# Attention scores with a stationary operand of 128 columns, and products of ones on TensorE until batch 0 is through

## The chip, the cores and the metric

The kernel runs on one core of a Trainium2 chip. The metric is the device time of one execution in microseconds (us). TensorE (PE in the profile) multiplies matrices: it loads a stationary operand (a row of its own, PEld) and streams a moving operand past it, into PSUM. VectorE (DVE), ScalarE (ACT) and GpSimd (POOL) do the rest, and DMA queues move data.

## The reference

For 8 batches, 12 heads, 448 positions and 64 elements per head: cosine attention, then a mixing block on the 448 x 768 result of each batch.

```python
q_n = q / (norm(q) + 1e-6);  k_n = k / (norm(k) + 1e-6)
attn = softmax(q_n @ k_n.T / tau)           # per batch and head
x = (attn @ v), heads side by side           # 448 x 768
u = x + ((x.T @ U) @ V).T                    # rank 32, over positions
out = u + relu(u @ w_ch1) @ w_ch2            # 768 -> 3072 -> 768
```

## The kernel before

All operands of products are bf16, sums are f32 in PSUM. PSUM is one tile `bank` of eight banks of 512 f32 columns. Positions are cut into four chunks of 112 (`SC`, `SCH`).

**Attention**, per batch and pair of heads (six pairs): q and k are loaded (L463), squared (L492 on ACT or L494 on DVE), summed (L498), turned into 1/norm (L511 to L519) and scaled into `xn` (L553). Batches 0 and 1 transpose `xn` on PE in groups of four chunks (`flip`, L443), with a copy of each group to `qkT` by ACT (L839) or DVE (L841); later batches use a DMA transpose. `qkT` holds 64 rows of one head and 64 of the other, eight chunks of 112 columns: four of q or k for the one side, four for the other. The scores (L587) take one chunk as the stationary operand (64 rows by 112 columns) against 448 columns of the other side, for both heads, so that a chunk is a pair of products on the two halves of the rows. Batch 0 plans them chunk by chunk, later batches in bursts of two chunks (`BURST`). ACT takes the exponential (L593) of both heads of a chunk into `attn`. The products with v (L607), 16 a head, have `attn` as the stationary operand and 65 columns of v, with a column of ones that gives the softmax's sum; DVE divides (L614, L616) into `X_sb`.

**Mixing**: X with U (L664, a stationary operand of 128 rows by 32 columns), with V (L643, L699, L745), a copy of X through PE in batch 0 (L638), then the products with the first weight matrix (L775, `w1_sb`), ReLU (L798, L800), those with the second (L809, `w2_sb`), the sum (L818) and the store (L832).

**Order.** Nothing is looped in order of batches. Every operation is an `Op` with a planned duration, dependencies and slots of rings that it takes and frees. `Plan.run` simulates the engines at build time. PE and POOL have ordered streams (for PE the streams `pe_tp`, `pe_first`, `pe_av`, `pe_a`, `pe_sc`, `pe_mlp`, in this order of preference), and whichever head is ready first in the plan is issued next; DVE, ACT and SP take by priority; copies and squares marked "ACT/DVE" go to the engine that the plan has free. So a planned duration that changes moves other work. The planned order is then the order in each engine's queue; semaphores do the waiting. PSUM banks 0 to 3 are two slots of scores (`r_sc`), banks 4 to 7 are shared by the rings `r_mm` (transposes and all mixing products, three at a time) and `r_av` (the products with v, two at a time). The first squares belong to heads 0 and 1 (on ACT), then 2 and 3, 4 to 7, 8 to 11.

Of the kernel before, what the change touches and what calls it, by code (L numbers as in the profile page):

```python
# [12 lines left out]
BF = mybir.dt.bfloat16  # L13
# [243 lines left out]
def kernel(  # L257
# [12 lines left out]
    nc = tc.nc  # L270

    B, H, S, D = q.shape
# [8 lines left out]
    SCH = S // SC  # L281
# [3 lines left out]
    PE_BATCHES = 2  # L285
    LATE, VLATE = 8.0, 3.2
    BURST = 2

    const = ctx.enter_context(tc.tile_pool(name="const", bufs=1))
    pool = ctx.enter_context(tc.tile_pool(name="pool", bufs=1))  # L290
# [58 lines left out]
    def bank_ring(groups, cap, shape=None):  # L349
        def make(g):  # L350
            if len(g) > 1:
                return bank_t[:, g[0]:g[-1] + 1, :]
            t_ = bank_t[:, g[0], :]
            if shape is not None:
                t_ = t_[:, 0:shape[0] * shape[1]].rearrange("p (a b) -> p a b", a=shape[0])
            return t_
        return BankRing(banks, groups, cap, make)

    r_mm = bank_ring([(7,), (6,), (5,), (4,)], 3)
    r_av = bank_ring([(4,), (5,), (6,), (7,)], 2, (4, D + 8))  # L360
    r_sc = bank_ring([(0, 1), (2, 3)], 2)
    r_sc1 = bank_ring([(0,), (2,), (1,), (3,)], 4)


# [17 lines left out]
        return ap.rearrange("(s c) d -> c s d", c=SC)[c, s0:s1]  # L382

    plan = Plan()
    pe_tp = plan.stream("PE")
    pe_first = plan.stream("PE")
    pe_av = plan.stream("PE")
# [5 lines left out]
    def pe_t(n):  # L393
        return n / 2400.0 + 0.0025
# [14 lines left out]
    def fill(fn, n=256, prio=8, acq=(), deps=()):  # L409
        return plan.add(Op("DVE", 0.05 + n * 0.0005, fn, deps=deps, acq=acq, prio=prio))  # L410
# [121 lines left out]
    def stats_first(ld, ops):  # L532
# [5 lines left out]
            ups.append(up)  # L538
        return ups + norm(0, 0, ld, 0, inv, 0, done, -1)

    def norm(b, p, ld, la, inv, a, deps, pr):


        by_pe = b < PE_BATCHES
        first = b == 0 and p == 0
        xn, qkT = Slot(r_xn, 2 if by_pe else 1), Slot(r_qkT, SC // (1 if b == 0 else BURST))

        def part(i):
            def fn():
                src = ld.tile[:, i, la:la + 2, :].rearrange("p h (c d) -> p h c d", d=D)  # L550
                sc = inv.tile[:, i, a:a + 2, :].unsqueeze(3).to_broadcast([SCH, 2, SC, D])
                dst = xn.tile[:, SC * (1 - i):SC * (2 - i), :].rearrange("p c (h d) -> p h c d", h=2)
                nc.vector.tensor_mul(dst, src, sc)  # L553
            return plan.add(Op("DVE", dve_t(512), fn, deps=[deps[i]], acq=[xn],
                               rel=[getattr(ld, "slot", ld), inv], prio=pr))

        ops = {i: part(i) for i in ((0, 1) if first else (1, 0))}
        if not by_pe:
            done = [plan.add(Op("SP", 0.1, lambda: nc.sync.dma_start_transpose(
                out=qkT.tile, in_=xn.tile.rearrange("p b e -> p (b e)")), deps=list(ops.values()), acq=[qkT],  # L560
                rel=[xn], prio=0, lat=("x", 0.05 * 56, LATE)))]
        else:
            done = []
            for i, o in ops.items():
                b0, b1 = SC * (1 - i), SC * (2 - i)
                done.append(flip(
                    pe_tp, [(lambda z=z: xn.tile[:, z, :]) for z in range(b0, b1)], SCH,
                    lambda: qkT.tile, (lambda t_, x, b0=b0, b1=b1: [(t_[:, b0:b1, :], x)]),
                    [o], [qkT], [xn], 1, "ACT/DVE", 0.09 if first else 0.05))
        got[b, p, "qkT"] = (qkT, done)  # L570
        return list(ops.values())


    def attention(b, p, X):
        off = PAD * (b % 2)
        qkT, qdeps = got.pop((b, p, "qkT"))
        attn = Slot(r_attn, 2)
        exps = []
        g = 1 if b == 0 else BURST
        for c0 in range(0, SC, g):  # L580
            scs = [Slot(r_sc, 1) for _ in range(g)]

            def score(scs=scs, c0=c0):
                for n, sc in enumerate(scs):
                    for hh in range(2):
                        r = slice(D * hh, D * hh + D)
                        nc.tensor.matmul(out=sc.tile[0:SCH, hh, 0:S], lhsT=qkT.tile[r, c0 + n, :],  # L587
                                         rhs=qkT.tile[r, SC:2 * SC, :].rearrange("p c s -> p (c s)"),
                                         start=True, stop=True)
            o = plan.add(Op("PE", (0.2 + pe_t(S) * g) * (1.8 if b == 0 and p < 2 else 1), score,  # L590
                            deps=qdeps, acq=scs, rel=[qkT]), pe_first if b == 0 else pe_sc)
            for n, sc in enumerate(scs):
                exps.append(plan.add(Op("ACT", act_t(2 * S, 0.08), lambda sc=sc, c=c0 + n: nc.scalar.activation(  # L593
                    out=attn.tile[:, c, :, off:off + S], in_=sc.tile[0:SCH, :, 0:S], func=AF.Exp,
                    scale=inv_tau), deps=[o], acq=[attn], rel=[sc], prio=0.1 if b == 0 else 1)))
        last_exp[b] = exps[-1]
        if b == 0 and p == 0:
            last_exp["first"] = [exps[0]]
        muls = []
        for hh in range(2):  # L600
            h = 2 * p + hh
            av, rd = Slot(r_av, 1), Slot(r_rd, 1)
            for t in range(4):
                for j in range(SC):
                    first, last = t == 0 and j == 0, t == 3 and j == SC - 1
                    def fn(t=t, j=j, h=h, hh=hh, av=av):
                        nc.tensor.matmul(  # L607
                            out=av.tile[:, t, 0:D + 1],
                            lhsT=attn.tile[:, j, hh, 128 * t:128 * (t + 1)],
                            rhs=v_t[b % 2][:, h, j, 0:D + 1], start=(j == 0), stop=(j == SC - 1))  # L610
                    o = plan.add(Op("PE", 0.09 if b == 0 and p == 0 else 0.033, fn,
                        deps=exps + got[b, h, "v"] + attn_set + [v_set[b % 2]] if first else (), acq=[av] if first else [],
                        rel=[attn] if last else []), pe_av)
            r = plan.add(Op("DVE", 0.20, lambda av=av, rd=rd: nc.vector.reciprocal(  # L614
                out=rd.tile, in_=av.tile[:, :, D:D + 1]), deps=[o], acq=[rd], prio=1))
            muls.append(plan.add(Op("DVE", dve_t(256), lambda av=av, rd=rd, h=h: nc.vector.tensor_mul(  # L616
                X.tile[:, :, h * D:(h + 1) * D], av.tile[:, :, 0:D],
                rd.tile.to_broadcast([128, 4, D])), deps=[r],
                acq=[X], rel=[av, rd], prio=1)))
        last_av[b, p] = o  # L620
        return muls
# [28 lines left out]
    def stage0(b, X, muls):  # L650
        par = b % 2
# [3 lines left out]
        A = Slot(r_A, 0)  # L655
# [3 lines left out]
        for c0, c1 in cols:  # L659
            mm = Slot(bank, 1)  # L660
            need = [m for i, m in enumerate(muls) if i * D < c1]
            for t in range(4):
                o = plan.add(Op("PE", pe_t(c1 - c0) + 0.2 if t == 0 else 0.01,
                                lambda t=t, c0=c0, c1=c1, mm=mm: nc.tensor.matmul(  # L664
                    out=mm.tile[R * t:R * (t + 1), 0:c1 - c0], lhsT=U_sb[:, par, t, :],
                    rhs=X.tile[:, t, c0:c1], start=True, stop=True),
                    deps=need + consts[:2 + par] if t == 0 else (), acq=[mm, A] if t == 0 else []),
                    pe_a if c1 < C else pe_av)
            a = Op("ACT/DVE", any_t(c1 - c0), None, deps=[o], rel=[mm], prio=0)
            a.fn = lambda a=a, c0=c0, c1=c1, mm=mm: copy_op(  # L670
                a, A.tile[:, c0:c1], mm.tile[:, 0:c1 - c0])
            a_done.append(plan.add(a))
            if b == 0:
                ut += [columns(X, A, uT, muls, cc, a) for cc in range(c0 // 128, c1 // 128)]
        tiles = range(3) if par == 0 else range(3, 7)
        n = 128 * len(tiles)
# [8 lines left out]
        for z, (c0, c1) in enumerate(cols):  # L685
            for i, t in enumerate(tiles):
# [7 lines left out]
                mm = Slot(bank, 1)  # L694
                for y, (AA, col) in enumerate(parts):
# [4 lines left out]
                        out=mm.tile[:, 0:c1 - c0], lhsT=V_sb[:, col:col + 128],  # L700
# [148 lines left out]
    def set_attn(t_):  # L849
        nc.vector.memset(t_[:, :, :, S:512].bitcast(mybir.dt.uint32), ones)  # L850

    attn_set = [fill(lambda t_=t_: set_attn(t_), 1000, prio=i - 2.5) for i, t_ in enumerate(attn_t)]

    def load_u(par):
# [89 lines left out]
        mlp(b, *state[b])  # L944

    order = plan.run()
    for o in order:
        for s in o.acq:
            if s.tile is None and not getattr(s, "own", False):
                s.tile = s.ring.make(s.group if isinstance(s.ring, BankRing) else s.i)  # L950
        o.fn()
# [33 lines left out]
```

## Time and profile before

| what | value |
|---|---|
| median of 13 runs | 602.39 us (600.6 to 603.99) |
| profiled execution | 601.95 us |
| its span in the trace | 600.1 us |
| PE busy | 581.3 us, 97% |
| DVE / ACT / POOL busy | 311.2 / 270.2 / 75.6 us |
| scores L587 | 384 products, 60.9 us busy |
| products with v, L607 | 1536 products, 60.5 us busy |
| L775 and L809 | 1152 and 1368 products, 233.4 and 231.2 us busy |

The span begins with the first instruction of any engine. A group's row in the profile names line, engine, operation, output<-inputs and shapes, then the count, busy time and mean duration of one; behind the second bar stands the idle time of the engine just ahead of the group, with what ended it. The duration of a product includes its way through the array, so products that follow one another closely overlap, and what a product costs PE is read from the distance between starts. In a timeline a row is a run of alike instructions: start, duration of the run, and how many.

### The profile page before, as it was taken

The page shows a single profiled execution, that of the slowest core. Times are in us where ns is not written, and L with a number is a line of the kernel's source. Part 1 is how long each engine was busy: PE and PEld are TensorE (multiplying, and loading weights), DVE is VectorE, ACT ScalarE, POOL GpSimd, SP SyncE. Part 2 cuts the span into 40 slices and gives each one's busy share as a digit, 9 for nine tenths or more (in the row PEclk, how much of TensorE's full clock was granted, in tenths as well). Part 3 has the DMA queues.
Part 4 walks back from the last instruction along what each step waited for, and adds up shares of the span by engine and source line. Part 5 has one row for each costly group of instructions (what it writes and reads, how often), then busy time and mean ns, then how long its engine had stood idle before and what let it go on. Part 6 is the DMA issues. An engine that isn't in the chain of part 4 may idle for free.

```text
span 600.1 us, 11347 instructions
## 1 busy us (share of the span) xinstructions
PE 581.3 (97%) x4725; PEld 328.7 (55%) x4725; DVE 311.2 (52%) x728; ACT 270.2 (45%) x425; POOL 75.6 (13%) x101
## 2 busy tenths in 40 slices
PE   3899999999999999999999999999999999999997
PEld 1555655544565555555445665555445666654565
DVE  7868949989988768767773243324320210110011
ACT  7777644566545556456661056604541024014300
POOL 6434220140310020030020000000000000000000
PEclk9999999999999999999999999999999999999999
DMA  9999993898795594895494121121002110310021
GB/s 144 212 201 193 209 130 69 134 112 121 83 172 97 88 108 63 141 127 82 61 78 82 54 58 29 26 71 40 2 1 55 51 40 1 90 43 1 0 54 54
DMA packets 132851, 50.66 MB, mean 84 GB/s; under 512 B 97728, under 2 KB 132800, under 8 KB 132800
## 3 DMA queue, kind: packets, MB, share of 16 engines
q0 software_dynamic: 71680, 25.73, 38.2%
q1 hardware_dynamic: 61056, 24.19, 20.5%
q8 instruction: 37, 0.61, 0.4%
q14 instruction: 14, 0.11, 0.1%
q10 hardware_dynamic: 64, 0.02, 0.0%
HBM read 52.25 MB, written 11.01 MB: 105 GB/s over the span
## 4 chain that ended last, share of the span: by engine, by line
PE 91%; DVE 4%; ACT 1%; DMA 1%; POOL 1%; issue 1%; DVEq 0%; POOLq 0%
PE bank L775 37%; PE bank L809 36%; PE bank L607 8%; PE bank L587 8%; PE bank L699 1%; DMA qk_nat<-in_q_dram 1%; ACT attn L593 1%; DVE xn L553 1%; PE bank L664 1%; PE bank L443 1%; POOL v_nat L472 1%; DVE u_nat L713 1%; POOL qk_nat L463 0%; DVE u_nat L710 0%; DVE relu L800 0%
## 5 line engine op out<-in xcount | busy, mean ns | idle before, releaser
L775 PE MATMUL bank<-uT,w_sb 128*128 128x512 bf16 (+1 forms) x1152 | 233.4, 353 | 1.3 <-DVE u_nat L710 0.7
L809 PE MATMUL bank<-w_sb,relu 128*128 128x384 bf16 (+1 forms) x1368 | 231.2, 323 | 0.6 <-DVE O_sb L818 0.3
L593 ACT ACTIVATE attn<-bank 112x896 bf16<-112x896 f32 x192 | 166.5, 916 | 131.7 <-PE bank L587 86.9
L809 PEld LDWEIGHTS <-relu 128*128 128x128 bf16 x1368 | 129.3, 98 | 91.5 <-issue 12.3
L775 PEld LDWEIGHTS <-w_sb 128*128 128x128 bf16 x1152 | 108.1, 98 | 111.0 <-issue 18.5
L798 ACT ACTIVATE relu<-bank 128x384 bf16<-128x384 f32 (+1 forms) x136 | 74.3, 547 | 131.8 <-PE bank L775 131.6
L818 DVE TENSOR_TENSOR O_sb<-bank,u_nat 128x384 f32<-128x384 f32 (+1 forms) x57 | 31.1, 549 | 173.2 <-PE bank L809 155.5
L498 DVE TENSOR_REDUCE ss<-sq 112x8 f32<-112x512 bf16 x96 | 63.2, 674 | 3.0 <-ACT sq L492 2.6
L587 PE MATMUL bank<-qkT 64*112 64x448 bf16 x384 | 60.9, 386 | 3.4 <-ACT attn L593 2.5
L607 PEld LDWEIGHTS <-attn 112*128 112x128 bf16 x1536 | 57.3, 99 | 11.3 <-issue 4.3
L553 DVE TENSOR_TENSOR xn<-qk_nat,inv 112x512 bf16<-112x512 bf16 x94 | 61.6, 687 | 0.2
L607 PE MATMUL bank<-v_nat,attn 112*128 112x65 bf16 x1536 | 60.5, 195 | 0.2 <-DVE uT L841 0.2
L800 DVE TENSOR_SCALAR relu<-bank 128x384 bf16<-128x384 f32 (+1 forms) x56 | 34.3, 612 | 32.1 <-PE bank L775 30.1
L616 DVE TENSOR_TENSOR X_sb<-bank,rd 128x256 bf16<-128x256 f32 x96 | 39.1, 417 | 1.5
L614 DVE RECIPROCAL rd<-bank 128x4 f32<-128x4 f32 x96 | 16.5, 176 | 42.6 <-PE bank L607 42.1
L463 POOL DMA_DIRECT2D qk_nat<-in_q_dram x24 | 17.1, 713 | 155.8 <-DVE xn L553 118.2
L472 POOL DMA_DIRECT2D v_nat<-in_v_dram x32 | 29.8, 942 | 53.0 <-PE bank L607 52.2
L494 DVE TENSOR_TENSOR sq<-qk_nat 112x512 bf16<-112x512 bf16 x88 | 34.2, 413 | 0.9 <-DMA qk_nat<-in_q_dram 0.8
L587 PEld LDWEIGHTS <-qkT 64*112 64x112 bf16 x384 | 18.7, 127 | 26.5 <-issue 22.6
L713 DVE TENSOR_TENSOR u_nat<-bank,X_sb 128x384 bf16<-128x384 f32 (+2 forms) x45 | 22.5, 526 | 17.9 <-PE bank L699 17.4
L443 PE MATMUL bank<-ident,xn 112*128 112x112 bf16 x96 | 10.3, 246 | 9.5 <-DVE xn L553 9.4
L463 POOL DMA_DIRECT2D qk_nat<-in_k_dram x24 | 16.8, 701 | 4.7 <-DMA w_sb<-in_moe_w_ch_dram 3.6
(46 smaller groups left out, 132.9 us busy)
## 6 DMA issues: line engine op xcount, KB each, us to landing
v_nat<-in_v_dram POOLq DMA_DIRECT2D x32, 168.0 KB, 6.6
qk_nat<-in_q_dram POOLq DMA_DIRECT2D x23, 224.0 KB, 6.0
qk_nat<-in_k_dram POOLq DMA_DIRECT2D x23, 224.0 KB, 6.6
w_sb<-in_moe_w_ch_dram POOLq DMA_DIRECT2D x4, 1152.0 KB, 15.4
w_sb<-in_moe_w_ch_dram POOLq DMA_DIRECT2D x8, 576.0 KB, 16.0
out_dram<-O_sb SPq DMA_DIRECT2D x15, 168.0 KB, 2.2
out_dram<-O_sb SPq DMA_DIRECT2D x16, 144.0 KB, 2.1
out_dram<-O_sb SPq DMA_DIRECT2D x16, 120.0 KB, 2.0
```

Source lines behind the costliest of these rows:

```text
L472: ops = [load(lambda c=c: nc.gpsimd.dma_start(out=v_t[b % 2][:, :, c, 0:D], in_=v[b].rearrange("h (s c) d -> c s h d", c=SC)[c]), SCH * H ...
L494: nc.vector.tensor_mul(y, x, x)
L498: lambda i=i, a0=a0, a1=a1, sq=sq: nc.vector.reduce_sum(ss.tile[:, i, a0:a1, :].rearrange("p h c -> p (h c)"), sq.tile[:, 0:a1 - a0, :].re ...
L553: nc.vector.tensor_mul(dst, src, sc)
L587: nc.tensor.matmul(out=sc.tile[0:SCH, hh, 0:S], lhsT=qkT.tile[r, c0 + n, :], rhs=qkT.tile[r, SC:2 * SC, :].rearrange("p c s -> p (c s)"), ...
L593: exps.append(plan.add(Op("ACT", act_t(2 * S, 0.08), lambda sc=sc, c=c0 + n: nc.scalar.activation(out=attn.tile[:, c, :, off:off + S], in_ ...
L607: nc.tensor.matmul(out=av.tile[:, t, 0:D + 1], lhsT=attn.tile[:, j, hh, 128 * t:128 * (t + 1)], rhs=v_t[b % 2][:, h, j, 0:D + 1], start=(j ...
L616: muls.append(plan.add(Op("DVE", dve_t(256), lambda av=av, rd=rd, h=h: nc.vector.tensor_mul(X.tile[:, :, h * D:(h + 1) * D], av.tile[:, :, ...
L775: o = plan.add(Op("PE", pe_t(n), lambda cc=cc: nc.tensor.matmul(out=mm.tile[:, 0:n], lhsT=w1_sb[:, cc, f * 128:(f + 1) * 128], rhs=uT.tile ...
L798: nc.scalar.activation(out=relu.tile[:, f, 0:n], in_=mm.tile[:, 0:n], func=AF.Relu)
L800: nc.vector.tensor_relu(out=relu.tile[:, f, 0:n], in_=mm.tile[:, 0:n])
L809: nc.tensor.matmul(out=mm.tile[:, 0:c1 - c0], lhsT=relu.tile[:, f, i * 128:(i + 1) * 128], rhs=w2_t[:, f, c0:c1], start=(f == 0), stop=(f ...
```

## The change

Three things change; everything else in the order follows from the planner.

- A score's stationary operand is 128 columns of the flat `qkT` from the chunk's first column on: 112 of the chunk, and 16 of the next one. The product writes 128 rows of PSUM instead of 112; the exponential still reads 112.
- `warm`, a 128 x 128 tile of ones set by DVE, is multiplied by itself into bank 4: 52 times as the first operation of PE's first stream (planned at 5.4 us), and, until the first product with U of batch 0, in every gap of PE's plan over 0.25 us, 70% of it at 0.056 us a product. In the built program there are 195 such products: 62 ahead of the first transpose, then groups of 7, 12, 12, 12, 5, 41, 12, 12, 4, 3, 3, 3 and 7. Bank 4 is kept by them until that product with U, and the products with v prefer banks 5 to 7.
- Planned durations lose what was added for the first pairs: transposes 0.05 us for 0.09, scores without the factor 1.8, products with v 0.033 for 0.09.

In the queues of the changed program, between the ninth and the 24th exponential of batch 0 ACT has no other work (before: three copies). Up to the end of batch 0's attention DVE has one square and three copies of `qkT` more, ACT as many less. Of the products of batch 0 with v, 30 stand in one run between the tenth and the eleventh score of the batch (before: 32), and later runs between scores have 10 to 22 (before: 14 to 18). Batches 1 to 7 have 84 bursts of four scores in both. POOL's queue is the same; in SP's some transposes change places.

```diff
+    FILL = 0.7
...
-    r_av = bank_ring([(4,), (5,), (6,), (7,)], 2, (4, D + 8))
+    r_av = bank_ring([(5,), (6,), (7,), (4,)], 2, (4, D + 8))
     r_sc = bank_ring([(0, 1), (2, 3)], 2)
+    r_warm = bank_ring([(4,)], 1)
...
+    pe_warm = plan.stream("PE")
     pe_tp = plan.stream("PE")
...
+    warm_t = const.tile([128, 128], BF, name="warm")
+    warm = Slot(r_warm, 1)
+
+    def warm_up(n):
+        for _ in range(n):
+            nc.tensor.matmul(out=warm.tile[:, 0:128], lhsT=warm_t, rhs=warm_t, start=True, stop=True)
...
-                    [o], [qkT], [xn], 1, "ACT/DVE", 0.09 if first else 0.05))
+                    [o], [qkT], [xn], 1, "ACT/DVE", 0.05))
...
+                flat = qkT.tile.rearrange("p b s -> p (b s)")
                 for n, sc in enumerate(scs):
                     for hh in range(2):
                         r = slice(D * hh, D * hh + D)
-                        nc.tensor.matmul(out=sc.tile[0:SCH, hh, 0:S], lhsT=qkT.tile[r, c0 + n, :],
+                        nc.tensor.matmul(out=sc.tile[:, hh, 0:S], lhsT=flat[r, SCH * (c0 + n):SCH * (c0 + n) + 128],
                                          rhs=qkT.tile[r, SC:2 * SC, :].rearrange("p c s -> p (c s)"),
                                          start=True, stop=True)
-            o = plan.add(Op("PE", (0.2 + pe_t(S) * g) * (1.8 if b == 0 and p < 2 else 1), score,
+            o = plan.add(Op("PE", (0.2 + pe_t(S) * g), score,
...
-                    o = plan.add(Op("PE", 0.09 if b == 0 and p == 0 else 0.033, fn,
+                    o = plan.add(Op("PE", 0.033, fn,
...
+                    rel=[warm] if b == 0 and c0 == 0 and t == 3 else []),
                     pe_a if c1 < C else pe_av)
...
+    warm_set = fill(lambda: nc.vector.memset(warm_t, 1.0), 128, prio=-20)
+    plan.add(Op("PE", 5.4, lambda: warm_up(52), deps=[warm_set], acq=[warm]), pe_warm)
...
     order = plan.run()
+    free, cool = None, False
     for o in order:
+        if o.by == "PE" and not cool:
+            if free is not None and o.start - free > 0.25:
+                warm_up(int((o.start - free - 0.12) * FILL / 0.056))
+            free, cool = o.start + o.dur, warm in o.rel
```

More of the change, by code (lines that the diff above doesn't have):

```diff
@@ L666, in stage0 @@
                     rhs=X.tile[:, t, c0:c1], start=True, stop=True),
-                    deps=need + consts[:2 + par] if t == 0 else (), acq=[mm, A] if t == 0 else []),
+                    deps=need + consts[:2 + par] if t == 0 else (), acq=[mm, A] if t == 0 else [],
+                    rel=[warm] if b == 0 and c0 == 0 and t == 3 else []),
                     pe_a if c1 < C else pe_av)
```

## The prediction

> **What bounds the kernel now.** I read the page's busy shares first, then its 40 slices, then the chain that ended last.
>
> ```profile
> PE 581.3 (97%) x4725; PEld 328.7 (55%) x4725; DVE 311.2 (52%) x728; ACT 270.2 (45%) x425; POOL 75.6 (13%) x101
> ...
> PE   3899999999999999999999999999999999999997
> ...
> PE bank L775 37%; PE bank L809 36%; PE bank L607 8%; PE bank L587 8%; PE bank L699 1%; DMA qk_nat<-in_q_dram 1%; ACT attn L593 1%; DVE xn L553 1%; PE bank L664 1%; PE bank L443 1%; POOL v_nat L472 1%; DVE u_nat L713 1%; POOL qk_nat L463 0%; DVE u_nat L710 0%; DVE relu L800 0%
> ```
>
> TensorE (PE) is busy in every slice but the first two, and the chain's large shares are its products. So from about 43 us (the first long run of L775 products) to the end, the time is the sum of what PE takes per product, and a saving there counts in full. By the list of waits for PE from 40 us on, PE waits only 0.7 + 0.3 + 0.3 + 0.2 + 0.2 + 0.2 = 1.9 us. Before 43 us another sum applies: batch 0's attention must be done before there is other work for PE.
>
> The page's clock row shows 9 from the first slice, but the groups of PE instructions, asked for 22 to 27.4 us and then for 27.4 to 30 us, show something else:
>
> ```profile
> L587 PE MATMUL bank<-qkT 64*112 64x448 bf16 x8 | 2.2, 607 | 0.0
> L607 PE MATMUL bank<-v_nat,attn 112*128 112x65 bf16 x32 | 1.9, 244 | 0.0
> ```
>
> ```profile
> L587 PE MATMUL bank<-qkT 64*112 64x448 bf16 x6 | 1.2, 393 | 0.0
> L607 PE MATMUL bank<-v_nat,attn 112*128 112x65 bf16 x26 | 1.2, 194 | 0.0
> ```
>
> The same products take 607 ns, then 393 ns. PE is slow until about 27.5 us and fast afterwards. The change's dense products end that stretch early.
>
> **Scores in the steady part.** PE's timeline around 300 us and around 136 us (start, duration, count):
>
> ```profile
> 299.72 0.38 PE L775 MATMUL bank<-uT,w_sb 128*128 128x512 bf16 x1
> 300.03 0.59 PE L587 MATMUL bank<-qkT 64*112 64x448 bf16 x4
> 300.55 3.19 PE L775 MATMUL bank<-uT,w_sb 128*128 128x512 bf16 x14
> ```
>
> ```profile
> 135.88 1.90 PE L775 MATMUL bank<-uT,w_sb 128*128 128x512 bf16 x8
> 137.71 0.35 PE L664 MATMUL bank<-X_sb,U_sb 128*32 128x384 bf16 x4
> 137.99 1.04 PE L775 MATMUL bank<-uT,w_sb 128*128 128x512 bf16 x4
> ```
>
> Fourteen L775 products of 512 columns take 3.19 us, one alone 0.38; so they start (3.19 - 0.38)/13 = 0.216 us apart. A score burst is two pairs of products of 448 columns, and the two of a pair run side by side (64 rows each). At that rate two pairs should take 2 x 0.216 x 448/512 = 0.378 us; from 300.03 to the next product they take 0.52, that is 0.142 more. And the product ahead of them holds PE for 0.31 instead of 0.216, 0.094 more. The excess of a burst is 0.236 us. Batches 1 to 7 have 7 x 6 x 2 = 84 bursts, so **19.8 us** lie in this excess. How much of it is the weight load?
>
> ```profile
> L607 PEld LDWEIGHTS <-attn 112*128 112x128 bf16 x1536 | 57.3, 99 | 11.3 <-issue 4.3
> L587 PEld LDWEIGHTS <-qkT 64*112 64x112 bf16 x384 | 18.7, 127 | 26.5 <-issue 22.6 <-ACT qkT L839 0.9 <-DVE qkT L841 0.4
> ...
> L664 PEld LDWEIGHTS <-U_sb 128*32 128x32 bf16 x72 | 1.9, 92 | 6.0 <-issue 6.0
> ```
>
> Columns: busy us, mean ns of one. A load of 128 columns (of 112 rows here) takes 99 ns, one of 112 columns 127, one of 32 columns 92. The full width is loaded in a shorter form, and the change gives the scores that width (their rows stay 64). What the long load costs is seen in L587's own durations, shortest 347 and median 393: the first pair of a burst waits for its load inside its duration, the second pair's load is hidden, 393 - 347 = 46 ns. The other 0.19 us stand ahead of the first product and behind the last. Do these go too? The L664 products say no: 8 x 0.216 = 1.73 us after 135.88 would be 137.61, and they start at 137.71, 0.10 late; 0.28 to the next product, where 384 columns need 0.162, is 0.12 of excess. Their load (92 ns) is shorter than the full one and they lose as much on both sides. What L664 and L587 share is a tile that is not the whole array (32 columns, 64 rows), and the changed scores still have 64 rows.
>
> The value I take: the full-width load leaves some 10 ns unhidden (46 less the 28 ns between the two load rows is 18; between 0 and 18), so **-35 ns a burst, 84 x 0.035 = -2.9 us**. The ends: the whole excess goes, -19.8 us; or the short form needs 128 rows as well, and 16 more columns cost (127 - 92)/80 x 16 = 7 ns, 84 x 0.007 = +0.6 us.
>
> The Trainium skill speaks on both sides, and nothing else here rests on it. "TensorE: Matmul & The Clock Gate", section "Weight-path perf modes", says that fast weight load is on when the number of weights is 128 and the type isn't FP32; the rows of 99 and 127 ns agree. "TensorEngine Tiling (Array Packing)", section "Key Properties", speaks against a large gain: "Changing tiling mode (not just tile) drains the TensorE". The 0.1 us on both sides of L664 and L587 fit a drain, and no run here separates them yet. By the second rule the sum is the one I take; if the loads alone made the excess, it would be -19.8.
>
> **The start.** What sets 43 us is ScalarE's (ACT) exponentials of batch 0, 24 in a row:
>
> ```profile
> 23.46 1.71 ACT L593 ACTIVATE attn<-bank 112x896 bf16<-112x896 f32 x2
> 26.16 0.92 ACT L593 ACTIVATE attn<-bank 112x896 bf16<-112x896 f32 x1 [0.98 <-PE bank L587]
> 26.97 0.53 ACT L839 COPY qkT<-bank 128x448 bf16<-128x448 bf16 x1
> 27.38 1.74 ACT L593 ACTIVATE attn<-bank 112x896 bf16<-112x896 f32 x2
> 28.99 0.56 ACT L839 COPY qkT<-bank 128x448 bf16<-128x448 bf16 x1
> 29.40 8.34 ACT L593 ACTIVATE attn<-bank 112x896 bf16<-112x896 f32 x10
> ```
>
> Ten take (8.34 - 0.96)/9 = 0.82 us from start to start. The ninth starts at 23.46, the 24th at 37.96: 14.5 us, where 15 x 0.82 = 12.3 would do. The 2.2 us between are a wait of 0.98 for a score that stood behind 32 slow L607 products, and copies (0.53, 0.56 and 0.50 at 37.60). In the changed order ACT has no copy between the ninth and the 24th: three qkT copies and one square have moved to VectorE (DVE), and PE is fast. Against it: the square that comes to DVE (about 0.4 us, row L494, 413 ns) stands ahead of the normalisation of heads 4 to 7, and DVE was busy 15.48 of 16.50 us from 6.9 to 23.4 us (the windows), so the ninth exponential comes some 0.4 later. And scores still stand behind L607 products in pieces of 30 and twice 22 (before: 32, then 14 to 18), 0.03 us each even when fast: some 0.5 us for these. 2.2 - 0.4 - 0.5 = **-1.3 us**. Ends: -2.2, and +0.5 if nothing comes back and DVE's extra work (three copies of 0.38 and the square, 1.55 us) finds no more cover than DVE's idle 16.50 - 15.48 = 1.02.
>
> The dense products themselves: 52 and 10 run before the first transpose, which waits for DVE until 6.90. Transposes of 112 columns are 0.093 us apart in the slow stretch, so 128 columns take 0.107; 62 x 0.107 = 6.6 us from about 1.1 us end at 7.7 if PE stays slow throughout, and before 6.9 if it turns fast halfway. At worst 0.8 us late, at nothing: the first eight exponentials have slack, since the ninth hangs on the load of heads 8 to 11, whose first square waits for its DMA until 16.01, and on DVE behind it. The 133 later products stand in gaps of PE's plan and fill 70% of each. A gap that isn't there costs up to 0.056 x 41 = 2.3 us in the longest, but it lies where PE waited for DVE (idle before L443, 9.4 us in all). All end before the first long L775 run. The memset of the ones (nearest row 98 ns, L847) lies in DVE's idle 2.64 us before 4.14; without that cover, 0.1. Bank 4 is kept from the other rings until the first U products; the three left were enough in the plan, and one wait for a bank would be 0.4 (39.37 was one of 0.25). From 43 us on the order of the work is also shuffled by the planner; the 1.9 us of waits can go or double: 0, between -1.9 and +1.9.
>
> **Sum.** The profiled execution took 601.95 us (span 600.1 and 1.85 around it), 0.44 under the median of 602.39. 601.95 - 2.9 - 1.3 = **597.8 us**. With the ends of the start and of the waits it goes from 601.95 - 2.9 - 2.2 - 1.9 = 594.9 to 601.95 - 2.9 + 0.5 + 1.9 = 601.5.
>
> **Rivals.**
> - *Width brings no short load with 64 rows.* For it: no row shows 64 rows with 128 columns. Against it: L607 with 112 rows has 99 ns, so full rows aren't needed. 601.95 - 1.3 + 0.6 = 601.3.
> - *One of the two 0.1 us sides goes too*, if it belongs to the long load: 84 x 0.096 = 8.1 more, 589.7. *Both go*: 601.95 - 19.8 - 1.3 = 580.9. L664 speaks against both.
> - *Slower: the pairs no longer run side by side.* Today the timeline shows four products in 0.52 us. If the short form keeps the second half's load from lying beside the first half's product, a pair takes another 0.187 us: 168 x 0.187 = 31.4, less 1.3 and 2.9, 629 us. It decides once (4.2 + 1.2)/0.187, about 29 of 168 pairs, run one after the other. Against it: in full tiles the short load already lies beside products (L775 at 0.216 a product).
>
> **How the numbers follow.** Forecast 0.62, no short load 0.14, one side 0.08, both sides 0.08, pairs apart 0.08. The range 589 to 602.3 holds the forecast, the one-sided case and most of the first rival, 0.81; the likeliest case's own range is 594.9 to 601.5. A measurement of this kernel can tell about 0.2% (1.2 us) from no change. Faster: 0.62 + 0.08 + 0.08 and 0.02 of the first rival, 0.80; within: 0.10 of it; slower: 0.08 + 0.02 = 0.10.
>
> **What would show it.** Score load row at about 98 ns with 128 columns; L587's successor with first pairs near 357 ns and pairs still together; excess of 0.20 a burst instead of 0.236; exponentials 9 to 24 without a copy between them, the 24th near 36.6; products at 393 ns from the first scores on. I am wrong if the 0.1 us on each side of a burst shrinks, if the load row stays above 120, or if DVE holds back the exponentials.

## The result and the profile after

The changed kernel takes 596.71 us in the median of 11 runs (595.5 to 599.05), the one before 602.52 us in 48 runs: a ratio of 0.990, 95% interval 0.9884 to 0.9915. The forecast was 597.8 us. The profiled execution of the changed kernel took 598.29 us (span 596.5), 1.6 us over its median; its span is 3.6 us under that of before. Seven of the 48 runs before lie apart from the rest, at 604.8 to 606.4 us; the ratios count them and the medians hardly do, so a ratio can show more gain than the two medians beside it.

From the page after: the busy row, the slices of PE and of its clock, and the two rows of the scores (busy us, mean ns of one).

```profile
PE 586.5 (98%) x4920; PEld 333.2 (56%) x4920; DVE 309.1 (52%) x729; ACT 270.0 (45%) x425; POOL 75.4 (13%) x101
...
PE   8899999999999999999999999999999999999997
...
PEclk9899999999999999999999999999999999999999
...
L599 PE MATMUL bank<-qkT 64*128 64x448 bf16 x384 | 55.5, 358 | 0.3 <-ACT attn L605 0.2
...
L599 PEld LDWEIGHTS <-qkT 64*128 64x128 bf16 x384 | 12.0, 94 | 22.3 <-issue 18.7
```

The load of the scores' operand takes 94 ns with 128 columns and 64 rows (127 with 112 columns), and the mean product 358 ns for 386. PE is still the bound. PE's timeline around a burst in the steady part of the changed kernel:

```profile
297.81 0.81 PE L788 MATMUL bank<-uT,w_sb 128*128 128x512 bf16 x3
298.56 0.55 PE L599 MATMUL bank<-qkT 64*128 64x448 bf16 x4
299.04 3.19 PE L788 MATMUL bank<-uT,w_sb 128*128 128x512 bf16 x14
```

Three L788 products need 3 x 0.216 = 0.65 us; the burst starts 0.75 after the first, 0.10 late as before. From the burst to the next product it takes 0.48 us, where it took 0.52.

What PE waits for from 43 us on. First the kernel before with the width alone (its order is that of before), then the changed kernel (columns: us in all, times, longest):

```profile
PE bank L776 <- DVE u_nat L711: 0.7, 1, 0.7
PE bank L810 <- DVE O_sb L819: 0.3, 1, 0.3
PE bank L776 <- DVE u_nat L714: 0.3, 1, 0.3
PE bank L810 <- DVE u_nat L711: 0.2, 1, 0.2
PE bank L776 <- DVE relu L801: 0.2, 1, 0.2
PE bank L700 <- DVE u_nat L714: 0.2, 1, 0.2
```

```profile
PE bank L822 <- DVE O_sb L831: 0.3, 1, 0.3
PE bank L788 <- ACT uT L852: 0.2, 1, 0.2
PE bank L712 <- DVE u_nat L726: 0.2, 1, 0.2
```

The waits for `u_nat` ahead of the products with the first weight matrix are gone. Counted as distance between starts beyond a product's own length, without the sides of bursts, PE loses 3.5 us after 43.5 us in the kernel before and 1.0 in the changed one, **2.5 us less**. The same count for the scores' 84 bursts: the second pair comes 0.041 us late before and 0.007 after, 2.8 us less, and the product ahead is held 0.0955 us for 0.0932, 0.2 more: **2.6 us less**. That is 5.1 us, 1.5 more than the span lost. The 2.5 us depend on where the count begins: the changed kernel has a wait of 0.4 us just before 43.5, and counted from 43.0 us on the waits are 2.0 us less. The difference, 1.0 to 1.5 us, is at the **start**:

```profile
22.81 0.36 PE L599 MATMUL bank<-qkT 64*128 64x448 bf16 x2
24.64 0.36 PE L446 MATMUL bank<-ident,xn 112*128 112x112 bf16 x4 [1.47 <-DVE X_sb L628]
24.93 0.36 PE L599 MATMUL bank<-qkT 64*128 64x448 bf16 x2
25.22 1.27 PE L619 MATMUL bank<-v_nat,attn 112*128 112x65 bf16 x30
26.42 0.56 PE L599 MATMUL bank<-qkT 64*128 64x448 bf16 x2
```

This is PE's timeline in the changed kernel. Four transposes wait 1.47 us for L628, which frees a bank of the products with v: bank 4 is held for the ones, the products with v hold two of the other three. The windows show what follows. Columns: stretch, its length, busy us of PE, PEld, DVE, ACT and POOL, and after the last bracket the granted clock, DMA share and GB/s.

```profile
5.60:26.00 20.40, 15.85 (x244) 12.11 (x242) 18.55 (x44) 14.71 (x28) 7.18 (x10) 1.00 1.57 197
26.10:29.40 3.30, 3.30 (x29) 1.80 (x26) 2.72 (x8) 2.00 (x3) 2.44 (x4) 0.50 0.66 107
29.50:42.00 12.50, 12.24 (x200) 8.12 (x200) 7.24 (x23) 11.36 (x15) 6.94 (x10) 1.00 1.18 178
```

PE was fast from 5.5 us on, at half the clock again from 26.0 to 29.4, and fast after that. ACT's timeline of the changed kernel gives the exponentials of batch 0; the ninth starts at 24.55 (before: 23.46), the 24th at 38.95 (before: 37.96):

```profile
24.55 1.73 ACT L605 ACTIVATE attn<-bank 112x896 bf16<-112x896 f32 x2
27.02 0.92 ACT L605 ACTIVATE attn<-bank 112x896 bf16<-112x896 f32 x1 [0.75 <-PE bank L599]
28.11 0.92 ACT L605 ACTIVATE attn<-bank 112x896 bf16<-112x896 f32 x1 [0.17 <-PE bank L599]
29.51 10.36 ACT L605 ACTIVATE attn<-bank 112x896 bf16<-112x896 f32 x12 [0.48 <-PE bank L599]
```

There is no copy between them any more, but ACT waits for scores instead. So the profile already says that the predicted sum came true with other parts: the width as forecast, the start not faster, and the waits behind it shorter.

### The profile page after: what moved, and what is told of

Same layout as the page of the kernel before. It is cut to its first block, busy times and chain, and to the rows that moved or that the text cites. A ratio compares the mean times of both kernels' runs of the same rounds, so it can differ in the third digit from the quotient of the medians.

```text
span 596.5 us, 11746 instructions
## 1 busy us (share of the span) xinstructions
PE 586.5 (98%) x4920; PEld 333.2 (56%) x4920; DVE 309.1 (52%) x729; ACT 270.0 (45%) x425; POOL 75.4 (13%) x101
## 4 chain that ended last, share of the span: by engine, by line
PE 93%; DVE 3%; DMA 1%; POOL 1%; ACT 1%; issue 0%; DVEq 0%; POOLq 0%
PE bank L788 37%; PE bank L822 37%; PE bank L619 8%; PE bank L599 7%; PE bank L712 1%; DMA qk_nat<-in_q_dram 1%; ACT attn L605 1%; PE bank L446 1%; PE bank L676 1%; DVE xn L564 1%; POOL v_nat L475 1%; POOL qk_nat L466 0%; DVE u_nat L726 0%; DVE ss L501 0%; DVE O_sb L831 0%
## 5 line engine op out<-in xcount | busy, mean ns | idle before, releaser
L788 PE MATMUL bank<-uT,w_sb 128*128 128x512 bf16 (+1 forms) x1152 | 232.9, 353 | 0.2 <-ACT uT L852 0.2
L788 PEld LDWEIGHTS <-w_sb 128*128 128x128 bf16 x1152 | 108.4, 98 | 110.5 <-issue 17.5
L619 PEld LDWEIGHTS <-attn 112*128 112x128 bf16 x1536 | 56.3, 98 | 11.3 <-issue 4.2
L599 PE MATMUL bank<-qkT 64*128 64x448 bf16 x384 | 55.5, 358 | 0.3 <-ACT attn L605 0.2
L628 DVE TENSOR_TENSOR X_sb<-bank,rd 128x256 bf16<-128x256 f32 x96 | 39.1, 416 | 1.3
L466 POOL DMA_DIRECT2D qk_nat<-in_q_dram x24 | 17.1, 712 | 154.2 <-DVE xn L564 145.4
L599 PEld LDWEIGHTS <-qkT 64*128 64x128 bf16 x384 | 12.0, 94 | 22.3 <-issue 18.7
L550 PE MATMUL bank<-warm 128*128 128x128 bf16 x195 | 15.6, 241 | 1.1 <-DVE warm L865 1.1
```

The lines of the kernel that those rows point to most:

```text
L466: ops = [load(lambda i=i, src=src: nc.gpsimd.dma_start(out=ld.tile[:, i, lo:lo + h1 - h0, :], in_=src[b, h0:h1].rearrange("h (s c) d -> s ...
L599: nc.tensor.matmul(out=sc.tile[:, hh, 0:S], lhsT=flat[r, SCH * (c0 + n):SCH * (c0 + n) + 128], rhs=qkT.tile[r, SC:2 * SC, :].rearrange("p ...
L619: nc.tensor.matmul(out=av.tile[:, t, 0:D + 1], lhsT=attn.tile[:, j, hh, 128 * t:128 * (t + 1)], rhs=v_t[b % 2][:, h, j, 0:D + 1], start=(j ...
L788: o = plan.add(Op("PE", pe_t(n), lambda cc=cc: nc.tensor.matmul(out=mm.tile[:, 0:n], lhsT=w1_sb[:, cc, f * 128:(f + 1) * 128], rhs=uT.tile ...
```

## The experiments

Theory after the result: the change is the width (2.6 us) plus a better order behind 43 us (2.5 us), and the early clock is worth little. Rivals: the early clock makes the second half; the sides of a burst belong to the load's form or to the scores as such; the ones cost more than they bring.

### The width alone

The kernel before with one edit:

```diff
-                        nc.tensor.matmul(out=sc.tile[0:SCH, hh, 0:S], lhsT=qkT.tile[r, c0 + n, :],
+                        nc.tensor.matmul(out=sc.tile[:, hh, 0:S], lhsT=flat[r, SCH * (c0 + n):SCH * (c0 + n) + 128],
```

> The kernel before with one edit: the scores' stationary operand is 128 columns. Order, banks and PE's slow start are those of before. Theory (only the unhidden part of the first load of a burst goes, the drain on both sides stays): a burst is 0.031 to 0.035 us shorter, 84 bursts, so 2.6 to 2.9 us faster, and PE slow until about 27 us as before. Rival (the gain of the change comes from the start and the new order): within 1 us of before. Rival (the wide load removes the drains in the old order): 10 us or more faster.

Measured: 599.7 us against 602.84 on the same chip, 3.1 us faster by the medians. The ratio, 0.9928 (0.9904 to 0.9952), is 4.3 us, because five of the 14 runs before on that chip lie at 605.1 to 605.7 us and none of the six with the width does. The second pair of a burst is 0.007 us late for 0.041, both sides are as before, the waits behind 43.5 us are 3.6 us. The first theory holds, and the time comes from the trace and not from the ratio alone: both sides of a burst stay.

### The change without the width

```diff
-                        nc.tensor.matmul(out=sc.tile[:, hh, 0:S], lhsT=flat[r, SCH * (c0 + n):SCH * (c0 + n) + 128],
+                        nc.tensor.matmul(out=sc.tile[0:SCH, hh, 0:S], lhsT=qkT.tile[r, c0 + n, :],
```

> The changed kernel with the scores' stationary operand back at 112 columns; products of ones, banks and order stay. Theory: slower than the changed kernel by 2.6 to 2.9 us, that is 3 us faster than before, from fewer waits of PE between 43 and 230 us and not from the start. Rival (all of the gain is the width): equal to before within 1 us.

Measured: 600.12 us, ratio 0.9942 (0.9918 to 0.9966), 2.7 us faster than before. The waits behind 43.5 us are 1.0 us, as in the changed kernel; the 24th exponential starts at 38.17, 0.3 us earlier than with the width alone (38.47), although PE was fast from 6.7 us on in this profile. By the medians the two halves of the change add up: 3.1 + 2.7 = 5.8.

### What makes the 0.1 us on each side of a burst

```diff
-                        r = slice(D * hh, D * hh + D)
+                        r = slice(0, 128)
```

> The changed kernel, but each score product contracts over all 128 rows, so that the scores of both heads are added up, a different computation with the same instructions and queues. The four products of a burst then run one after the other. Theory (the 0.1 us on each side of a burst is the change from a full tile to 64 rows and back): both sides vanish, the product ahead of a burst is back at its own length and a burst takes 4 x 0.189 = 0.76 us, 0.18 more than the 0.57 of the changed kernel, 84 x 0.18 = 15 us slower. Rival (the 0.1 us belongs to the scores' products as such, their operands or their waits): the sides stay, 0.95 us a burst, 31 us slower.

PE's timeline of this run (three rows around a burst):

```profile
297.73 1.67 PE L788 MATMUL bank<-uT,w_sb 128*128 128x512 bf16 x7
299.24 0.92 PE L599 MATMUL bank<-qkT 128*128 128x448 bf16 x4
300.00 0.38 PE L788 MATMUL bank<-uT,w_sb 128*128 128x512 bf16 x1
```

Seven products need 7 x 0.216 = 1.51 us, and the burst starts 1.51 after them; four score products need 4 x 0.189 = 0.756, and the next one starts 0.76 later. Both sides are gone (0.2 ns in the median of 84). The one run took 612.12 us, 15 over the median of the changed kernel and 14 over its profiled run, as worked out.

The same with 112 columns:

> As the run with all 128 rows, but the stationary operand has 112 columns: full rows with the long form of the load; the scores of both heads are added up here too. Theory (the tile's shape makes the sides, the form of the load adds only its own unhidden part): loads near 124 ns, the sides at most 0.03 us each. Rival (a change between the two forms of the load costs the 0.1 us): about 0.1 us on each side, although the rows are full.

```profile
299.82 0.59 PE L788 MATMUL bank<-uT,w_sb 128*128 128x512 bf16 x2
300.25 0.92 PE L599 MATMUL bank<-qkT 128*112 128x448 bf16 x4
301.01 3.40 PE L788 MATMUL bank<-uT,w_sb 128*128 128x512 bf16 x15
```

Two products need 0.43, the burst starts 0.43 after them and takes 0.76. Its loads take 131 ns each and are hidden; the sides are 0.2 ns. The one run took 613.33 us, of which a slow stretch of PE at the start (16.3 to 19.8 us) is a part. So the sides belong to the step between full rows and 64 rows, and the form of the load has no part in them. This is what the Trainium skill's page "TensorEngine Tiling (Array Packing)", section "Key Properties", calls a drain at a change of tiling mode; it gives no time, and here it is 0.093 to 0.096 us in each direction, 84 x 0.19 = 16 us of this kernel.

### The ones without bank 4

The changed kernel with the products of ones in columns 448 to 511 of bank 0, which no score uses, two of 64 columns for each of 128; the products with v prefer bank 4 again, and the planner has four banks.

```diff
-    r_av = bank_ring([(5,), (6,), (7,), (4,)], 2, (4, D + 8))
+    r_av = bank_ring([(4,), (5,), (6,), (7,)], 2, (4, D + 8))
...
-    r_warm = bank_ring([(4,)], 1)
+    r_warm = Ring(1, lambda i: bank_t[:, 0, S:512])
...
-            nc.tensor.matmul(out=warm.tile[:, 0:128], lhsT=warm_t, rhs=warm_t, start=True, stop=True)
+            nc.tensor.matmul(out=warm.tile, lhsT=warm_t, rhs=warm_t[:, 0:64], start=True, stop=True)
```

> The changed kernel, but the products of ones go to the 64 columns of a score bank that no score uses (two products of 64 columns for one of 128), so bank 4 is not held and the products with v prefer banks 4 to 7 as before; the planner orders with four banks. Theory (holding bank 4 leaves the transposes without a bank at 23 to 24.6 us, a wait of 1.5 us in which PE falls back to the slow clock): that wait is gone, no slow stretch after the first, the 24th exponential 1 to 2 us earlier, 1 to 2 us faster than the changed kernel. Rival (the ninth exponential hangs on DMA and DVE alone, the bank does not matter): equal within 0.7 us.

Measured: 597.14 us, ratio 0.9901 (0.988 to 0.9921): equal to the changed kernel, as the rival has it. But the trace shows two things at once. The wait for the bank is gone and PE stays fast; the twelfth exponential starts 2.4 us after the ninth (changed kernel 3.6). What this gains is lost afterwards, by a wait that the edit itself brings in:

```profile
31.00 0.36 PE L599 MATMUL bank<-qkT 64*128 64x448 bf16 x2
32.44 0.39 PE L550 MATMUL bank<-warm 128*128 128x64 bf16 x8 [1.07 <-ACT attn L605]
32.76 0.36 PE L599 MATMUL bank<-qkT 64*128 64x448 bf16 x2
```

The ones wait, on a semaphore, for an exponential that reads bank 0, though in other columns, and the next score, whose own slot (banks 2 and 3) was free from 31.35 on, stands behind them until 32.76. So this run does not settle what the bank costs; a later one comes closer.

### Ones at the head only

The changed kernel with 52 products of ones and none in the gaps:

```diff
-    FILL = 0.7
+    FILL = 0.0
```

> The changed kernel with the 52 products of ones at the head alone; none in the gaps of the plan. Order and banks stay. Theory (the later products keep the clock up in gaps of 2 to 3 us, and lie in time that PE waits anyway): PE is slow again from about 20 us on for a part of batch 0's attention, 0 to 2 us slower than the changed kernel. Rival (they delay PE, since 143 of them follow a plan that the chip does not keep): 1 to 2 us faster.

Measured: 597.85 us, ratio 0.9915 (0.9894 to 0.9936), some 1 us above the changed kernel by the ratios (0.0015), which the intervals do not tell from no difference. PE's clock by the windows is 1.00 from 4.4 to 11.1 us, 0.50 from 11.3 to 28.1, and 1.00 again. The head alone doesn't keep the clock up. But the 24th exponential starts at 38.59, no later than in the two profiles of the changed kernel (38.95 and 38.68): for the start, the products in the gaps aren't shown to bring more than the head does.

### The order of before with ones

The kernel before with the width, and after its planning:

```diff
+    nc.vector.memset(warm_t, 1.0)
+    warm_up(52)
```

with the ones in the spare columns of bank 0; then the same with ones in the gaps of the old plan too.

> The kernel before with the 128 columns and with 52 products' worth of ones at the head (in spare columns of a score bank), with the planned durations, banks and order of before and nothing in the gaps. Theory (an early fast clock is worth little by itself, since batch 0's exponentials hang on DMA and DVE; what the changed kernel gains beside the width is its order): 0 to 1 us faster than the kernel with the width alone. Rival (the clock makes the gain): as fast as the changed kernel, 2 to 3 us faster than the width alone.

> As the run before it, with products of ones in the gaps of the old plan as well, up to the first product with U: the width and the clock of the changed kernel with the order and banks of before. Theory: the clock stays up, 0 to 1.5 us faster than with the head alone. Rival (order does not matter): equal to the changed kernel within 0.7 us.

Measured: 600.12 us (ratio 0.9956, 0.9939 to 0.9973) with the head, and 602.29 us (0.9995, 0.9974 to 1.0016) with the gaps as well. The head, expected to bring 0 to 1 us, brings nothing over the width alone (599.7 us, 0.9928): the clock is up from 6.4 to 9.8 us only. The products in the gaps were expected to gain and cost about 2 us. Again they stand in a score bank, and by the list of waits they waited 5.8 us for exponentials, 1.4 at the longest; the 24th exponential starts at 40.62. The expectation of the last run failed, and with this placement it says nothing on gaps that don't wait.

### The late products of ones

The changed kernel, and the one with the spare columns, without the products that the plan puts behind 25 us:

```diff
-            if free is not None and o.start - free > 0.25:
+            if free is not None and o.start - free > 0.25 and free < 25:
```

> The changed kernel without the last five groups of products of ones (4, 3, 3, 3 and 7), which the plan puts behind 25 us; the first 175 stay. Theory (these lie ahead of scores whose bank is free already, and put the 13th to 24th exponential at 0.91 us from start to start where 0.86 was seen without them): the 24th exponential 0.5 us earlier against the ninth, 0.3 to 0.8 us faster than the changed kernel. Rival (they lie in idle time): equal within 0.3 us.

> The kernel with the ones in spare columns of a score bank (bank 4 free), without its last four groups (4, 4, 4 and 7 products' worth, behind 25 us). Theory: its 13th to 24th exponential took 1.0 us each, with scores behind products of ones; without them 0.86, so the 24th exponential 1.2 to 1.7 us earlier against the ninth, 1 to 1.5 us faster than with them, near 595.8 us. Rival (bank 4 and the late products do not matter): 597 us as before.

With them on the same chip, the changed kernel again, and the changed kernel without any product of ones:

```diff
-        for _ in range(n):
+        for _ in range(0):
```

> The changed kernel itself once more, on the chip of these three, since the differences are under 1 us. Both: 596 to 597.5 us. A second profile shows whether the slow stretch at 26 to 29.4 us and the wait of 1.5 us for a bank ahead of it come each time. Theory: the wait comes each time, since it follows from the order; the slow stretch comes in a part of the executions.

> The changed kernel with its 128 columns, its planned durations, banks and order, but with no product of ones at all; the memset of the ones stays. PE is slow until about 27 us as before. Theory (what the change gains beside the width is its order, 2.5 us of waits less between 43 and 230 us): 596.9 to 598.3 us, within 1.2 us of the changed kernel and 1.5 to 3 us faster than the width alone. Rival (the early clock makes it): 599.5 us or more, like the width alone.

| on one chip, before 603.06 us | median us (range) | ratio, 95% interval |
|---|---|---|
| changed kernel again | 597.61 (596.13 to 598.18) | 0.9896, 0.9866 to 0.9928 |
| without the late ones | 597.57 (595.52 to 598.01) | 0.9899, 0.9869 to 0.9928 |
| spare columns, without the late ones | 595.24 (593.79 to 596.51) | 0.9864, 0.9834 to 0.9894 |
| no ones at all | 598.94 (598.6 to 600.12) | 0.9930, 0.9904 to 0.9955 |

*Without the late ones* the rival is right: no difference, although the 24th exponential starts 13.5 us after the ninth for 13.7. *With the spare columns* the theory is right: 2.4 us faster than the changed kernel beside it, the fastest version of this study. Its exponentials, by ACT's timeline:

```profile
24.42 1.71 ACT L605 ACTIVATE attn<-bank 112x896 bf16<-112x896 f32 x2
26.81 11.62 ACT L605 ACTIVATE attn<-bank 112x896 bf16<-112x896 f32 x14 [0.67 <-PE bank L599]
```

The 24th starts at 37.52, 13.1 us after the ninth, 14 in one run. That profile had a slow stretch of PE as well (23.0 to 26.5 us) and took 596.51 us, its slowest run. With bank 4 free and no late ones, the first long run of products with the first weight matrix starts at 42.01 us, for 42.95 without the late ones and 43.52 in the changed kernel beside it. So 0.9 to 1.5 of the 2.4 us are seen in the profiles. They belong to the free bank together with the order that the planner makes of four banks; the two were not taken apart.

*The changed kernel again* waits for L628 too (1.2 us in two waits, 1.0 the longest). Its slow stretch lies elsewhere, from 16.1 to 19.6 us, ahead of the wait; and the kernel with the spare columns has a slow stretch without any wait for L628. So the wait for a bank isn't shown to make PE slow. Nor does it come each time with this order: without the late ones its longest is 0.6 us, and with the ones at the head alone there is none. The median of 597.61 is just outside the 596 to 597.5 expected.

*Without ones* both statements miss: 598.94 is 0.6 above what the theory allowed and 0.6 below the rival. The trace says why. The waits behind 43.5 us are 1.5 us, the order's gain; but the exponentials of batch 0 (ACT's timeline) run into a PE that is slow until 34.0 us (a pair of scores takes 0.55 us up to there, 0.36 after):

```profile
25.81 0.92 ACT L605 ACTIVATE attn<-bank 112x896 bf16<-112x896 f32 x1 [0.23 <-PE bank L599]
28.06 0.92 ACT L605 ACTIVATE attn<-bank 112x896 bf16<-112x896 f32 x1 [1.34 <-PE bank L599]
29.14 2.70 ACT L605 ACTIVATE attn<-bank 112x896 bf16<-112x896 f32 x3 [0.16 <-PE bank L599]
32.61 0.92 ACT L605 ACTIVATE attn<-bank 112x896 bf16<-112x896 f32 x1 [0.77 <-PE bank L599]
```

and the 24th starts at 40.78, 2.3 us later than with the old order and the width (38.47). The ones bring it back to 38.68 and 38.95, and those at the head alone to 38.59. So the theory "the clock is worth little" falls for the new order. The new order takes 2 us off the waits and adds 2 us to the start; the ones undo what it adds.

## Why the prediction was right, and where it was not

- **The width: right.** -2.9 us was forecast, -2.6 is in the trace, -3.1 in the medians of the run with the width alone. The unhidden part of a first load fell from 0.041 to 0.007 us, and the product ahead is held 0.002 us longer, which the prediction did not have. The load row went to 94 ns, so the short form needs no full rows, and the first rival is out.
- **The sides of a burst stay: right**, and the reason taken from the U products, a tile that isn't the whole array, is now shown for the scores by the two runs with full rows. The rivals of one or both sides are out. The pairs still run side by side.
- **The start: wrong.** The step "2.2 - 0.4 - 0.5 = -1.3 us" failed. The 24th exponential, forecast near 36.6 us, came at 38.95, 0.99 us later than in the profile of before and 0.3 to 0.5 later than with the old order and the width (38.47 and 38.66). Four things took the place of the gain. (a) The ninth came 1.1 us later for 0.4: in all new-order runs it starts at 24.0 to 25.3, but with the old order too it was at 24.0 to 24.4 in every profile but the one predicted from, whose first square of heads 8 to 11 met its data at 16.01 where the others have 16.5 to 17.4. Of the 1.1 us, 0.6 is that early DMA, a draw of the one profile, and 0.3 the square that moved to DVE. (b) The bank: "one wait for a bank would be 0.4", held at nothing, was 1.47 and 1.04 us at its longest. (c) The clock: I let the ones keep PE fast, and it fell back for 3.4 us in both profiles of the changed kernel; what makes it fall there is not shown. (d) The pieces of products with v and the transposes ahead of scores: in the second profile of the changed kernel the 11th and 15th exponential come 1.33 and 1.20 us after the one before, for 0.8, 0.9 us in all where 0.5 was set aside.
- **The waits behind 43 us: mis-sized.** "0, between -1.9 and +1.9" was -2.5 us by distance between starts (-2.0 if counted from 43.0 us on), -1.2 by the list of waits.
- **The sum** came out 1.1 us above the median because two errors have opposite signs: the start 1.5 us slower in the profiled execution for 1.3 faster, the waits 2.5 us shorter for none. That they nearly cancel is luck; of the terms, only the width was right in size. Of the changed kernel's runs, those with a granted clock of 1.000 over the whole run took 595.6 to 596.7 us, those with 0.997 or less 597.5 to 599.1, and the two at 0.999 595.5 and 597.2. This clock leaves out the slow stretch ahead of its first record: the kernel before has 1.000 and is slow until 27.5 us.
- **The rival "slower"** had no part in it. What could have made the change slower was not on the list: the new order without a fast clock.

What stays open: how much of the 2.5 us of waits each of the planner's moves brings. The planned durations, the held bank and the preference for banks were not taken apart. Why seven runs of the kernel before took 604.8 us or more stays open too; no profile is of such a run.

## What to carry to other kernels

A stationary operand of the full 128 columns, even with columns that nobody reads, takes the load's long form away; but its worth is only that of the loads that nothing hides, here one pair in two. A change between full rows and 64 rows costs its 0.09 us each way whatever the load, so it is the number of such changes that should fall. Products that only keep PE awake need a place that no one else holds or reads: a bank taken from a ring, or columns beside an operand that another engine reads, gave back a part or all of what the clock brought here. Whether products behind the first 52 bring anything is not shown.

## What the runs showed of the hardware

- PE's clock falls back without a full stop. With 52 products at the head and the order of before it was up from 6.4 to 9.8 us and then fell, although PE had run 18 products (1.47 us busy) between 6.5 and 9.7; with the new order and no products in the gaps it fell at 11.2 us after 41 products (3.18 of 6.7 us busy). The fast and slow stretches that ended inside the first 40 us lasted 3.4, 6.8, 10.2, 17.1 or 20.5 us in these traces, multiples of 3.41 us.
- The drain between tile shapes is longer in the slow clock: with the pairs of the first 27 us of before, the step from transposes to scores costs 0.138 us beyond the transposes' own length, where the step from full products to scores costs 0.093 in the fast clock.
- A product that writes columns of a bank which no other instruction uses still waited for ACT's read of that bank's other columns, up to 1.07 us in the profile with the spare columns. The wait is on a semaphore of the program; whether the chip would need it, no run shows.
